# One of sixteen attention heads gets its transposes from VectorE in 32x32 blocks and its V product from 32-row matmuls

## The chip, the cores and the metric

The kernel runs on one core of a Trainium2 chip. The metric is device time in microseconds (us) of one execution, as the median of several runs. Engines: TensorE (PE for matmuls, PEld for weight loads), VectorE (DVE), ScalarE (ACT), GpSimd (POOL) and SyncE (SP), which issues most transfers.

## The reference, cut to what matters

Attention over 2 x 8 = 16 heads with 768 positions and 64 features each, masked by six-bit hash buckets, feeds two MLP stages. Only the attention is touched.

```python
mask = q_bucket[:, :, :, None] == k_bucket[:, :, None, :]
scores = np.where(mask, scale * np.matmul(q, k.transpose(0, 1, 3, 2)), -1000000000.0)
attn = np.exp(scores - np.max(scores, axis=-1, keepdims=True))
attn = attn / (np.sum(attn, axis=-1, keepdims=True) + 1e-09)
return np.matmul(attn, v).astype(np.float32)
```

## The kernel before, in words

The attention runs over 96 tiles, n = 0 to 95: six tiles of 128 queries for each head h = n // 6. For a tile, `t_qk` (lines 378 and 381) makes 128 x 768 scores with four matmuls into one of two PSUM tiles `s_ps`; the hash buckets enter through twelve extra rows of the operands `qb` and `hi`, so that unequal buckets become a large number. `t_max` (line 388, VectorE) clips the scores, takes the row extreme and writes the tile `p`; there are three of those. `t_exp` (line 400, ScalarE) takes exponentials in place and their row sum. `t_tr` (line 408, TensorE) transposes `p` in six blocks of 128 x 128 into two of the three PSUM banks `t` (`t_ps` twice and `pj_ps`), and `t_out` (line 417, ScalarE or VectorE) copies each bank into `pt`, keys on the partitions.

Three tiles make a group g of 384 queries, two groups a head. `block` runs once a group: `g_pv` (line 426) multiplies `pt` by V with six matmuls of 64 output rows, three into the upper half of the bank `u_ps` and three into the lower half, which `g_copy` (lines 448 and 451) takes out and `g_fold` adds up with transfers. Each 32-bit matmul shows in the profile as two instructions. In every second group `block` first makes the hash bits of the head two further on: two matmuls (line 352), two VectorE instructions `bits_rows` (line 359) right behind, and then a transfer `kb` (line 341, `hi<-q`), without which the scores of that head can't start.

TensorE's order in the attention is written out by hand in `names`: for each tile n the transposes of n, then the scores of n+3; behind the first tile of a group the V product of the group before. So `pv11` (with the bits of head 7) follows the scores of tile 39, and `pv13` (with the bits of head 8) the scores of tile 45; the scores of tile 48 are the first of head 8. The order on the other engines comes from a planner, `Work.run`, which simulates all engines at build time: it takes the task that could start first, and among those ready within 0.1 us (0.5 us on SP) the one with the earliest due time. Its prices and due times are the numbers in the `task` calls. Slots (`raw_s`) stand for buffers. Weight slices for the MLP are prepared by VectorE and ScalarE (`w_tick`, lines 201 to 224) wherever the planner finds room late in the attention.

Numbered by their order on the engines, tile 36 is the first of head 6: the scores of tile 39 start at 94.78 us in the profiled execution, those of tile 45 at 108.11 us and those of tile 48 at 115.16 us.

Of the kernel before, what the change touches and what calls it, by code (L numbers as in the profile page):

```python
# [18 lines left out]
DM, DF1, DF2 = 512, 768, 2048  # L19
NK = S // 128  # L20
CH = 256
HALF = S // 2
# [90 lines left out]
def lsh_attention_moe_kernel(  # L113
    ctx: ExitStack,
    tc: tile.TileContext,
    kq: bass.AP,
    v: bass.AP,
    pj: bass.AP,
    pc: bass.AP,
# [140 lines left out]
    def attention(mlp_steps):  # L260
        with ExitStack() as ax, ExitStack() as sx:
# [3 lines left out]
            p_p = ax.enter_context(tc.tile_pool(name="p", bufs=3))  # L265
            pt_p = ax.enter_context(tc.tile_pool(name="pt", bufs=3))
            sm_p = ax.enter_context(tc.tile_pool(name="sm", bufs=2))
# [11 lines left out]
            def load_head(h, parts=1):  # L279
                r = raw_p.tile([128, S], F32, tag="r", name="r")  # L280
                for i in range(parts):
                    cs = slice(i * S // parts, (i + 1) * S // parts)
                    nc.sync.dma_start(out=r[:, cs], in_=kq[h, :, cs])
                    if parts > 1 and i == 0:
                        nc.sync.dma_start(out=pj_raw, in_=pj)
                head[h] = dict(r=r)

            def load_v(h):
                vr = v_p.tile([128, NK, D], F32, tag="vr", name="vr", bufs=3)
                nc.sync.dma_start(out=vr, in_=v[h])  # L290
                head[h]["vr"] = vr

# [120 lines left out]
            def t_out(n, half, bank, copy):  # L413
                g, r = divmod(n, 3)
                if g not in grp:
                    grp[g] = pt_p.tile([128, NK, HALF], F32, tag="pt", name="pt")
                copy(  # L417
                    out=grp[g][:, 3 * half:3 * half + 3, r * 128:(r + 1) * 128],
                    in_=t_ps[bank.at][:, 0:HALF].rearrange("p (j q) -> p j q", j=3),
                )  # L420

# [133 lines left out]
            raw_s["vr"] = Slots(3)  # L555
# [41 lines left out]
            def bits_task(h, rows, due):  # L597
                q, ql, kh = moves[h]
                ready[h] = [task("SP", 0.8, due, prep_move, h, "kb", after=rows + [q], lag=2.5), q, ql, kh]

            def v_tasks(h):
                due = NK * h - 2
                vr = place("vr", 2)
                v_place[h] = vr
                if h > 0:
# [7 lines left out]
            def tile_tasks(n):  # L613
                h, t = divmod(n, NK)
                g, r = divmod(n, 3)
                sp, pp = place("s", 1), place("p", 2)
# [3 lines left out]
                if r == 0:  # L620
                    pt_p_[g] = place("pt", 1)
# [17 lines left out]
            def group_tasks(g, outs):  # L639
# [20 lines left out]
                )  # L660

            def pair_tasks(p_):
                due = 12 * p_ + 14
# [15 lines left out]
            for n in range(NT_):  # L679
                h, t = divmod(n, NK)  # L680
                if t == 0:
                    if h == 0:
                        v_tasks(0)
                        head_tasks(1)
                    if h + 2 < NH:
                        head_tasks(h + 2)
                    if h + 1 < NH:
                        v_tasks(h + 1)
                outs += tile_tasks(n)
                if n % 3 == 2:  # L690
# [6 lines left out]
            for g in range(NT_ // 3):  # L697
                for n in range(3 * g, 3 * g + 3):
                    names += [f"tr{n}", f"qk{n + 3}"]
                    if n == 3 * g and g:  # L700
                        names += [f"pv{g - 1}"] + ([f"rows{g // 4 - 1}"] if g % 4 == 2 else [])
            line = [t for x in names for t in order.get(x, ())]
# [249 lines left out]
```

## Time and profile before

| | us |
|---|---|
| median of 3 runs | 693.76 |
| lowest and highest | 693.68, 693.9 |
| the profiled execution | 694.73 |
| its span, first to last instruction | 693.0 |

The span is what the trace shows; the time of the same execution is 1.73 us longer and holds what lies around it. The runs without a profile lie about 1 us below the profiled one. The attention fills the span from about 9 to 232 us, the MLP the rest.

### The profile page before, as it was taken

Reading aid. Unit: us, or ns where it says so; the run is one execution under the profiler, and the core shown is the slowest. Engines: PE = TensorE matmul, PEld = TensorE weight load, DVE = VectorE, ACT = ScalarE, POOL = GpSimd, SP = SyncE. Lnnn points to the kernel's source line nnn. Section 1 sums busy time; section 2 is a strip of 40 time slices with the busy share of each in tenths; the row PEclk is TensorE's granted clock in tenths of the full one; section 3 lists DMA queues with packets and bytes.
Section 4 is the critical chain, followed back from the end, with each engine's and each line's share of the span. In section 5 each row is a group of like instructions: output and inputs, shape, how many; then the busy total and the mean of one; then the engine's idle time right before and its main releaser. Section 6 shows DMA issues by size and latency. Waiting matters only on the chain.

```text
span 693.0 us, 9878 instructions
## 1 busy us (share of the span) xinstructions
PE 683.4 (99%) x3516; PEld 541.3 (78%) x3516; DVE 491.3 (71%) x758; ACT 344.9 (50%) x669; POOL 273.0 (39%) x248
## 2 busy tenths in 40 slices
PE   7999999999999999999999999999999999999998
PEld 4777777677767688888888888888888888888886
DVE  6778787787776586775444356765888888888844
ACT  3777677777768333332322233665454444554430
POOL 4234564654730334443232112534434434434430
PEclk9999999999999999999999999999999999999999
DMA  5656576475541322221112022121111112211104
GB/s 157 131 135 142 138 195 159 115 177 140 141 101 39 107 92 91 92 92 53 47 45 69 31 70 88 56 78 45 61 61 62 61 61 66 85 62 61 31 0 183
DMA packets 26281, 62.76 MB, mean 91 GB/s; under 512 B 3940, under 2 KB 10692, under 8 KB 26232
## 3 DMA queue, kind: packets, MB, share of 16 engines
q1 hardware_dynamic: 26200, 62.12, 31.6%
q8 instruction: 28, 0.46, 0.3%
q14 instruction: 21, 0.17, 0.1%
q0 software_dynamic: 32, 0.00, 0.0%
HBM read 42.04 MB, written 3.19 MB: 65 GB/s over the span
## 4 chain that ended last, share of the span: by engine, by line
PE 94%; DVE 4%; ACT 1%; issue 1%; DMA 0%; DVEq 0%; ACTq 0%
PE b L746 47%; PE b L873 19%; PE u_ps L426 8%; PE t_ps L408 6%; PE s_ps L378 4%; PE s_ps L381 4%; PE pj_ps L408 3%; DVE p L388 1%; PE t_ps L352 1%; PE pj_ps L352 1%; DVE q L359 1%; DVE pt L417 1%; DVE lo L312 0%; ACT p L400 0%; DMA r<-in_kq 0%
## 5 line engine op out<-in xcount | busy, mean ns | idle before, releaser
L746 PE MATMUL b<-x_hl,w 128*128 128x512 f32 (+1 forms) x900 | 202.0, 381 | 0.0
L746 PEld LDWEIGHTS b<-x_hl,w 128*128 128x128 f32 x900 | 163.9, 188 | 33.1 <-issue 0.6
L773 POOL TENSOR_TENSOR g<-r,g 128x512 fp32r<-128x512 f32 x48 | 62.5, 1303 | 121.3 <-ACT g L772 121.3
L873 PE MATMUL b<-w,g 128*128 128x512 f32 (+1 forms) x438 | 105.9, 386 | 0.0
L388 DVE TENSOR_SCALAR_CACHE_REDUCE p<-s_ps 128x768 f32<-128x768 f32 x96 | 91.6, 956 | 15.8 <-PE s_ps L381 13.8
L400 ACT ACTIVATE p<-p,nm 128x768 f32<-128x768 f32 x96 | 90.1, 939 | 17.9 <-DVE p L388 16.9
L873 PEld LDWEIGHTS b<-w,g 128*128 128x128 f32 x438 | 81.5, 188 | 16.7
L230 POOL TENSOR_TENSOR w<-wg,w 128x512 fp32r<-128x512 f32 (+1 forms) x42 | 59.4, 1414 | 84.4 <-ACT w L224 68.6
L203 DVE SCALAR_TENSOR_TENSOR wg<-wg,wr 128x512 f32<-128x512 f32 (+1 forms) x58 | 66.1, 1140 | 35.6 <-ACT wg L201 34.8
L746 PE MATMUL b<-x_hl,wx 128*128 128x512 f32 x360 | 84.0, 389 | 0.0
L224 ACT CAST w<-wg 128x512 fp32r<-128x512 f32 (+1 forms) x42 | 25.5, 606 | 117.2 <-DVE wg L216 117.2
L746 PEld LDWEIGHTS b<-x_hl,wx 128*128 128x128 f32 x360 | 67.6, 188 | 14.0
L378 PE MATMUL s_ps<-lo,q 128*128 128x384 f32 x192 | 73.2, 381 | 3.5 <-DVE p L388 2.4
L426 PE MATMUL u_ps<-pt,vr 128*64 128x384 f32 x384 | 69.0, 491 | 0.2 <-DVE pt L417 0.2
L381 PE MATMUL s_ps<-hi,q 76*128 76x384 f32 x192 | 65.5, 341 | 0.7 <-DVE hi L343 0.7
L853 DVE SCALAR_TENSOR_TENSOR r<-r,b 128x512 f32<-128x512 f32 x48 | 33.0, 687 | 44.2 <-ACT r L852 44.2
L880 DVE TENSOR_TENSOR acc<-b,acc 128x512 f32<-128x512 f32 (+1 forms) x85 | 56.3, 675 | 7.7 <-PE b L873 7.6
L408 PE MATMUL t_ps<-ident,p 128*128 128x128 f32 x384 | 58.7, 275 | 0.3
L208 DVE TENSOR_SCALAR wg<-wg 128x512 int32<-128x512 int32 (+1 forms) x58 | 53.8, 927 | 2.8
L851 ACT ACTIVATE r<-b,half_sb 128x512 f32<-128x512 f32 x48 | 33.0, 687 | 41.3 <-PE b L746 41.3
L408 PEld LDWEIGHTS t_ps<-ident,p 128*128 128x128 f32 x384 | 45.8, 141 | 9.1 <-issue 4.8
L216 DVE SCALAR_TENSOR_TENSOR wg<-wr,wg 128x512 int32<-128x512 int32 (+1 forms) x58 | 51.7, 892 | 1.0
(87 smaller groups left out, 898.1 us busy)
## 6 DMA issues: line engine op xcount, KB each, us to landing
wr<-in_w SPq DMA_DIRECT2D x48, 512.0 KB
r<-in_kq SPq DMA_DIRECT2D x15, 384.0 KB
q<-hi SPq DMA_DIRECT2D x15, 384.0 KB
vr<-in_v SPq DMA_DIRECT2D x16, 192.0 KB
rb<-d SPq DMA_DIRECT2D x16, 192.0 KB
wr<-in_w SPq DMA_DIRECT2D x8, 384.0 KB
q<-lo SPq DMA_DIRECT2D x15, 192.0 KB
lo<-hi SPq DMA_DIRECT2D x15, 192.0 KB
```

What stands on the lines that cost most here:

```text
L203: nc.vector.scalar_tensor_tensor(out=f32(g), in0=f32(g), scalar=TINY_SQ, in1=f32(high), op0=ALU.is_ge, op1=ALU.mult)
L230: nc.gpsimd.tensor_tensor(out=w[:, 1, 0:cols], in0=f32(g2), in1=f32(w[:, 0, 0:cols]), op=ALU.subtract)
L378: nc.tensor.matmul(out=o, lhsT=hd["qa"][:, qs], rhs=hd["lo"][:, ks], start=True, stop=False)
L381: nc.tensor.matmul(out=o, lhsT=hd["qb"][0:76, qs], rhs=hd["hi"][0:76, ks], start=False, stop=True)
L388: nc.vector.tensor_scalar(out=p.rearrange("p (a k) -> p a k", a=2), in0=s_ps[n % 2][:, :, 0:HALF], scalar1=MASKED, scalar2=MASKED, op0=ALU ...
L400: nc.scalar.activation(out=p, in_=p, func=ACTF.Exp, scale=-1.0, bias=tl[n]["nm"], accum_out=pair[h // 2]["sums"][:, c:c + 1],)
L408: nc.tensor.transpose(out=t_ps[bank.at][:, j * 128:(j + 1) * 128], in_=tl[n]["p"][:, kt * 128:(kt + 1) * 128], identity=ident,)
L426: nc.tensor.matmul(out=u_ps[rows, 0:HALF], lhsT=vr[:, kt, :], rhs=grp[g][:, kt, :], start=(i == 0), stop=(i == 2),)
L746: nc.tensor.matmul(out=outp, lhsT=w_[a], rhs=x_[b_], start=(i == 0 and jj == 0), stop=(i == n - 1 and jj == 2),)
L773: nc.gpsimd.tensor_tensor(out=dst[:, 1, cs], in0=src, in1=f32(dst[:, 0, cs]), op=ALU.subtract)
L873: nc.tensor.matmul(out=pb[:, cs], lhsT=gs[f][:, a, tsl], rhs=wt[:, b_, cs], start=(n == 0), stop=(n == len(terms) - 1),)
L880: nc.vector.tensor_tensor(out=acc[:, t, cs], in0=pb[:, cs], in1=acc[:, t, cs], op=ALU.add)
```

## The change: what it does

For head 6 alone (`TURNED`), VectorE transposes each tile `p` of exponentials in 32x32 blocks into a new tile `dt` (`t_turn`): the blocks stay in their 32 partitions, so each quarter of the partitions holds the keys of its own 32 queries of every tile. The head's six tiles then have no `t_tr` and no `t_out`. V of that head is loaded once for each quarter (`v4`, 24 blocks of 32 keys, in all four quarters; 768 KB in place of 192 KB). `block4` makes the V product with 96 matmuls of 32 rows, 64 output columns and 192 moving columns: four quarters, each into a bank of its own (`u_ps` and the three `t` banks), even blocks into the upper and odd ones into the lower half. It comes in two parts, `b1` and `b2`; `b2` ends with the hash bits of head 8 as four matmuls of 192 columns into the free columns of two of the banks, and `rows4` takes those out in four instructions. `copy4` empties the four banks.

On TensorE `b1` stands behind the transposes of tile 42 and the scores of tile 45, `b2` behind the scores of tile 46 and ahead of the transposes of tile 43. The small transposes `rows` of each pair of heads move two tiles later. To make room, `pt` goes from three buffers to two, and V tiles of the other heads from three to two.

```diff
+            TURNED = (6,)
-                vr = v_p.tile([128, NK, D], F32, tag="vr", name="vr", bufs=3)
+                vr = v_p.tile([128, NK, D], F32, tag="vr", name="vr", bufs=2)
+            def load_v4(h):
+                vr = v_p.tile([128, NB, D], F32, tag="v4", name="v4", bufs=1)
+                nc.sync.dma_start(out=vr, in_=v4[h])
+            def t_turn(n):
+                nc.vector.transpose(out=head[h]["dt"][:, :, t * 32:(t + 1) * 32], in_=tl[n]["p"])
+            def block4(h, part, banks, bits):
+                for kb in range(part * NB // 2, (part + 1) * NB // 2):
+                    cols = UP if kb % 2 == 0 else DOWN
+                    for q in range(4):
+                        rows = slice(32 * q, 32 * q + 32)
+                        nc.tensor.matmul(
+                            out=b4_bank(banks[q])[cols, 0:NK * 32], lhsT=vr[rows, kb, :], rhs=dt[rows, kb, :],
+                            start=kb < 2, stop=kb >= NB - 2,
+                        )
+                if part and bits:
+                    for c in range(2):
+                        for half in range(2):
+                            nc.tensor.matmul(
+                                out=b4_bank(banks[c])[64 * half:64 * half + 64, 192:384], lhsT=pj_raw,
+                                rhs=head[bits]["r"][:, half * HALF + c * 192:half * HALF + c * 192 + 192], start=True, stop=True,
+                            )
+            def rows4(h, c, half, bank):
+                nc.vector.tensor_scalar(
+                    out=head[h]["qb"][64:108, at:at + 192], in0=b4_bank(bank)[rows, 192:384],
+                    scalar1=pc_sb[rows, 0:1], scalar2=pc_sb[rows, 1:2], op0=ALU.is_gt, op1=ALU.mult,
+                )
-            raw_s["pt"], raw_s["t"] = Slots(3), Slots(3)
+            raw_s["pt"], raw_s["t"] = Slots(2), Slots(3)
+                if turned:
+                    vready[h] = task("SP", 0.6, due - 2, load_v4, h, takes=[vr], lag=5.0)
+                if turned:
+                    return [task("DVE", 0.9, n - 4, t_turn, n, after=[ex], takes=[pt_p_[g]] if t == 0 else [], leaves=[pp])]
+                b1 = task("PE", 2.4, 6 * h + 8.4, block4, h, 0, banks, 0, after=outs + [vready[h]], takes=banks)
+                b2 = task(
+                    "PE", 3.4 if bits else 2.4, 6 * h + 8.4, block4, h, 1, banks, bits, after=[b1] + ([scaled[bits]] if bits else []),
+                names += [f"qk{n + 3}", f"pv{2 * h - 1}", f"tr{n}"] if after and t == 1 else [f"tr{n}", f"qk{n + 3}"]
+                if r == 0 and g and not (t and h in TURNED):
+                    names += [f"pv{2 * h - 2 if after and t == 0 else g - 1}"]
+                if g % 4 == 2 and t == 2:
+                    names += [f"rows{g // 4 - 1}"]
```

## Rows read from the trace of the kernel before

**Rows 1.** The page: busy us, share of the span and instructions by engine.
```profile
PE 683.4 (99%) x3516; PEld 541.3 (78%) x3516; DVE 491.3 (71%) x758; ACT 344.9 (50%) x669; POOL 273.0 (39%) x248
```

**Rows 2.** The page: the chain that ended last, shares of the span by engine.
```profile
PE 94%; DVE 4%; ACT 1%; issue 1%; DMA 0%; DVEq 0%; ACTq 0%
```

**Rows 3.** Timeline of PE about pv11: start, us, engine, line, instructions merged.
```profile
94.20 0.49 PE L408 MATMUL pj_ps<-ident,p 128*128 128x128 f32 x3
...
94.78 0.42 PE L378 MATMUL s_ps<-lo,q 128*128 128x384 f32 x1
...
95.66 0.87 PE L352 MATMUL t_ps<-r,pj_raw 128*64 128x384 f32 x4
96.35 2.10 PE L426 MATMUL u_ps<-pt,vr 128*64 128x384 f32 x12
98.39 0.55 PE L408 MATMUL pj_ps<-ident,p 128*128 128x128 f32 x3
```

**Rows 4.** Timeline of PE from the bits of head 8 to its first scores.
```profile
109.00 0.87 PE L352 MATMUL pj_ps<-r,pj_raw 128*64 128x384 f32 x4
...
112.42 0.42 PE L378 MATMUL s_ps<-lo,q 128*128 128x384 f32 x1
...
113.21 0.82 PE L408 MATMUL t_ps<-ident,p 128*128 128x128 f32 x6
...
115.16 0.42 PE L378 MATMUL s_ps<-lo,q 128*128 128x384 f32 x1
```

**Rows 5.** Timeline of DVE in head 6: start, us; in brackets idle time before.
```profile
88.15 0.96 DVE L388 TENSOR_SCALAR_CACHE_REDUCE p<-s_ps 128x768 f32<-128x768 f32 x1
...
89.03 0.56 DVE L417 COPY pt<-t_ps 128x384 f32<-128x384 f32 x1
89.50 0.95 DVE L388 TENSOR_SCALAR_CACHE_REDUCE p<-s_ps 128x768 f32<-128x768 f32 x1
...
94.41 0.96 DVE L388 TENSOR_SCALAR_CACHE_REDUCE p<-s_ps 128x768 f32<-128x768 f32 x1 [0.41 <-PE s_ps L381]
...
96.63 1.37 DVE L359 TENSOR_SCALAR q<-t_ps,pc_sb 44x384 fp32r<-44x384 f32 x2 [0.79 <-ACT p L400]
```

**Rows 6.** Windows: length, busy us (instructions) by engine, granted clock, DMA share, GB/s.
```profile
13.00:16.00 3.00, 1.54 (x9) 0.80 (x6) 2.92 (x5) 1.03 (x2) 1.60 (x2) 1.00 0.36 75
...
16.00:18.00 2.00, 1.54 (x10) 1.15 (x9) 1.97 (x5) 1.55 (x3) 0.00 (x0) 1.00 0.91 300
...
20.00:22.00 2.00, 2.00 (x17) 1.97 (x16) 1.70 (x4) 2.00 (x6) 0.62 (x1) 1.00 0.96 196
...
121.00:131.00 10.00, 8.54 (x55) 5.87 (x54) 9.36 (x17) 6.60 (x14) 7.70 (x10) 1.00 0.61 139
```

**Rows 7.** Groups by line and form: busy us, mean ns of one, idle before.
```profile
L388 DVE TENSOR_SCALAR_CACHE_REDUCE p<-s_ps 128x768 f32<-128x768 f32 x96 | 91.6, 956 | 15.8 <-PE s_ps L381 13.8 <-PE t_ps L408 0.6 <-ACT p L400 0.6
...
L426 PE MATMUL u_ps<-pt,vr 128*64 128x384 f32 x384 | 69.0, 491 | 0.2 <-DVE pt L417 0.2
...
L312 DVE SCALAR_TENSOR_TENSOR lo<-r,sc_sb,hi 128x384 fp32r<-128x384 f32 x4 | 3.7, 973 | 4.1 <-ACT hi L307 4.1
...
L343 DVE CAST q<-hi 64x384 fp32r<-64x384 f32 x2 | 0.7, 356 | 0.1
```

**Rows 8.** Timeline of SP's queue: issues of a V tile and of moves.
```profile
14.96 0.43 SPq L290 DMA_DIRECT2D vr<-in_v  x1
...
17.11 0.50 SPq L341 DMA_DIRECT2D lo<-hi  x1
...
99.57 0.59 SPq L462 DMA_DIRECT2D u<-uo  x1
...
111.37 0.80 SPq L341 DMA_DIRECT2D hi<-q  x1
```

**Rows 9.** Timeline of POOL: the sum that waits for that move.
```profile
101.89 1.01 POOL L471 TENSOR_TENSOR u<-u,uc 128x384 f32<-128x384 f32 x1 [1.76 <-DMA u<-uo]
```

**Rows 10.** Timeline of PE: the first scores of head 1.
```profile
21.66 0.42 PE L378 MATMUL s_ps<-lo,q 128*128 128x384 f32 x1
```

More of the change, by code (lines that the diff above doesn't have):

```diff
@@ L20 @@
 NK = S // 128
+NB = S // 32
 CH = 256
@@ L419, in t_out, with b4_bank, copy4 @@
                     in_=t_ps[bank.at][:, 0:HALF].rearrange("p (j q) -> p j q", j=3),
+                )
+            def t_turn(n):
+                h, t = divmod(n, NK)
+                if t == 0:
+                    head[h]["dt"] = pt_p.tile([128, NB, NK * 32], F32, tag="dt", name="dt", bufs=1)
+                nc.vector.transpose(out=head[h]["dt"][:, :, t * 32:(t + 1) * 32], in_=tl[n]["p"])
+            def b4_bank(b):
+                return u_ps if b.slots is raw_s["u_ps"] else t_ps[b.at]
+            def block4(h, part, banks, bits):
+                dt, vr = head[h]["dt"], head[h]["vr"]
+                for kb in range(part * NB // 2, (part + 1) * NB // 2):
[14 more added lines that the diff above has]
+            def rows4(h, c, half, bank):
+                rows = slice(64 * half, 64 * half + 44)
+                at = half * HALF + c * 192
+                nc.vector.tensor_scalar(
+                    out=head[h]["qb"][64:108, at:at + 192], in0=b4_bank(bank)[rows, 192:384],
+                    scalar1=pc_sb[rows, 0:1], scalar2=pc_sb[rows, 1:2], op0=ALU.is_gt, op1=ALU.mult,
+                )
+            def copy4(h, q, bank, copy):
+                pr = pair[h // 2]
+                if q == 0:
+                    pr["u"] = nm_p.tile([128, S], F32, tag="u", name="u")
+                copy(
+                    out=pr["u"].rearrange("p (t g k) -> p t g k", t=NK, g=4)[:, :, q, :],
+                    in_=b4_bank(bank)[:, 0:NK * 32].rearrange("p (t k) -> p t k", t=NK),
                 )
@@ L615, in tile_tasks @@
                 g, r = divmod(n, 3)
-                sp, pp = place("s", 1), place("p", 2)
+                turned = h in TURNED
+                sp, pp = place("s", 1), place("p", 1 if turned else 2)
                 tb = [place("t", 1) for i in range(2)]
@@ L619, in tile_tasks @@
                     sums_p[h // 2] = place("sums", 1)
-                if r == 0:
+                if turned and t == 0:
+                    pt_p_[g] = place("dt", 1)
+                elif r == 0:
                     pt_p_[g] = place("pt", 1)
@@ L660, in group_tasks, with turned_tasks @@
                 )
+            def turned_tasks(h, outs):
+                bits = h + 2 if h + 2 < NH else 0
+                banks = [place("u_ps", 3 if bits else 1)] + [place("t", 3 if bits and i == 0 else 1) for i in range(3)]
+                b1 = task("PE", 2.4, 6 * h + 8.4, block4, h, 0, banks, 0, after=outs + [vready[h]], takes=banks)
+                b2 = task(
+                    "PE", 3.4 if bits else 2.4, 6 * h + 8.4, block4, h, 1, banks, bits, after=[b1] + ([scaled[bits]] if bits else []),
+                    leaves=[pt_p_[2 * h], v_place[h]] + ([r_place[bits]] if bits else []),
+                )
+                order[f"pv{2 * h}"], order[f"pv{2 * h + 1}"] = [b1], [b2]
+                if bits:
+                    rows = [
+                        task("DVE", 0.45, 6 * h + 6, rows4, bits, c, half, banks[c], after=[b2], leaves=[banks[c]])
+                        for c in range(2) for half in range(2)
+                    ]
+                    bits_task(bits, rows, 6 * bits - 3)
+                u_p[h // 2], uc_p[h // 2] = place("u", 2), place("uc", 2)
+                cps = []
+                for q in range(4):
+                    ways = [("ACT", 0.43, nc.scalar.copy), ("DVE", 0.36, nc.vector.tensor_copy)]
+                    cps.append(task(*ways[0][:2], 6 * h + 5, copy4, h, q, banks[q], ways[0][2], after=[b2] + cps[:1], takes=[u_p[h // 2]] if q == 0 else [], leaves=[banks[q]]))
+                    work.also(*ways[1][:2], lambda a=(h, q, banks[q], ways[1][2]): copy4(*a), cps[-1])
+                for g in (2 * h, 2 * h + 1):
+                    adds[g] = task("SP", 0.5, 6 * h + 6, g_fold, g, after=cps, takes=[uc_p[h // 2]] if g % 2 == 0 else [], lag=3.5)
             def pair_tasks(p_):
@@ L696, in attention @@
             names = ["qk0", "qk1", "bits", "qk2"]
[L697 to L701, printed above, removed]
+            for n in range(NT_):
+                g, r = divmod(n, 3)
+                h, t = divmod(n, NK)
+                after = h - 1 in TURNED
+                names += [f"qk{n + 3}", f"pv{2 * h - 1}", f"tr{n}"] if after and t == 1 else [f"tr{n}", f"qk{n + 3}"]
[3 more added lines that the diff above has]
+                    names += [f"rows{g // 4 - 1}"]
             line = [t for x in names for t in order.get(x, ())]
```

24 lines of the change are left out of this document (16 added, 8 removed).

## The prediction, made before the changed kernel ran

> **What bounds the kernel now.** I read the page's busy times first: TensorE is busy 99% of the span, VectorE 71% [rows 1]. The chain that ended last is TensorE for 94% [rows 2]. So time saved on TensorE counts, if nothing else takes its place, and VectorE is the engine with the least room beside it. Then I read TensorE's and VectorE's timelines about head 6. TensorE goes from transposes to scores to V product without a gap: six transposes take 0.58 us (94.20 to 94.78), the bits of a head 0.69 us (95.66 to 96.35), a V product 2.04 us (96.35 to 98.39) [rows 3], the scores of a tile 0.79 us (112.42 to 113.21) [rows 4]. VectorE runs close on its heels: the check of tile 38 starts when its scores end, after 0.41 us of idling [rows 5]. Last I read the windows: from 121 to 131 us TensorE is busy 8.54 of 10 us while VectorE is busy 9.36 [rows 6]. Here, where VectorE also prepares weights, TensorE already waits for it, 1.46 us in all.
>
> **TensorE's account.** Removed are six tiles of transposes, 6 x 0.58 = 3.5 us, and two V products, 2 x 2.04 = 4.1 us: 7.6 us. The bits stay at the same number of columns, 0.7 us. Added are 96 matmuls of half the columns, 192 instructions. The trace shows no matmul of 32 rows, so I bound them. In the V product 12 instructions take 2.04 us though one lasts 491 ns [rows 3, 7]; the upper and the lower half run side by side, six pairs of 0.34 us. At half the columns a pair takes 0.17 us. If all eight parts of the array (four quarters, two halves) run side by side, each has 24 instructions one after the other: 24 x 0.17 = 4.1 us. If only the two halves do and the quarters queue, it is 96 x 0.17 = 16.3 us. I take 4.6 us, near the lower end, because the nearest row has its two parts fully side by side; 2.3 us for each part. TensorE's own account then gains 3.0 us, which would be 690.8.
>
> [...]
>
> **What TensorE waits for instead.** For head 6 TensorE has only scores to make, and scores wait for free `s_ps`, so for VectorE's checks. On VectorE a check holds the engine 0.88 us (88.15 to 89.03), a copy 0.47 us (89.03 to 89.50) [rows 5]. A turn is not in the trace. Bounds: twice the cheapest 384-column row from SBUF to SBUF, 2 x 0.356 = 0.71 us, and twice the dearest, 2 x 0.973 = 1.95 us [rows 7]. I take 0.88 us, that of the check, which has the same 128 x 768 elements. So VectorE gives up copies (at most two a tile, one on average since ScalarE shares them) and takes a turn.
>
> Count from 94.41 us, where the check of tile 38 starts [rows 5]. `b1` stands behind the scores of tile 45, which need the check of tile 43, and needs all six turns. VectorE owes six checks (5.3 us), five turns (4.4 us; I let the first one fall into idle time before), the bits of head 7 (1.37 us) and the wait ahead of them that is there now (0.79 us) [rows 5]: 11.9 us, up to 106.3. The scores of tile 45 take it to 107.1. TensorE alone would be there at 103.1: its V product would end 0.58 us earlier, at 97.8, then six scores, 4.7 us, and one tile's transposes, 0.58 us. So some 4 us of waiting appears where 7.6 us of work is taken out: the work on TensorE is moved behind VectorE instead of beside it.
>
> Behind it: `b1` to 109.4, scores of tile 46 to 110.2, `b2` to 112.5, bits of head 8 to 113.2.
>
> **The next wait is the key bits of head 8.** Now the bits start at 109.00 and the first scores of head 8 at 115.16 [rows 4]. Between them lie 6.2 us. In the changed order the bits are the last of `b2`, and only the transposes of tiles 43, 44 and 45 (1.7 us) and the scores of tile 47 (0.8 us) stand between. The chain beside it: the rows begin 0.97 us after the bits start (95.66 to 96.63) [rows 3, 5], so at 113.5. Four instructions of half the columns cost between 0.34 us (half of 0.68) and 0.68 us each; I take 0.45, nearer the half: 115.3. Then the move. Its issue follows the rows at once now (111.37) [rows 8], and a similar move took 2.3 us from issue to the first instruction that uses it (99.57 to 101.89) [rows 8, 9]. That is 117.6 for the scores of tile 48. TensorE alone, with 0.5 us for a bank to be emptied behind `b2`, would be there at 116.3. So TensorE waits 1.3 us more, and tile 48 stands at 117.6 where it stood at 115.16: 2.4 us late.
>
> **The start.** The planner has room for one more V tile ahead (14.96, V of head 2) [rows 8]. With two buffers that tile must wait, and the load of `v4` has no condition, so it takes that place: 768 KB for 192 KB, 590 thousand bytes more. At 196 to 300 GB/s [rows 6] that is 2.0 to 3.0 us more in a queue that is busy 0.91 to 0.96 of those windows. Behind it stands the last move for head 1, issued at 17.11 [rows 8], and head 1's first scores start at 21.66 [rows 10]. With 2.3 us for a move there are 2.2 us to spare, so the scores come between 0 and 0.8 us late; I take 0.3.
>
> **What is given back.** VectorE and ScalarE run up to two tiles ahead during `b1` and `b2`, and the weight steps that cost TensorE 1.46 us between 121 and 131 us [rows 6] may slip there. Between 0 and 1.46; I take half, 0.7.
>
> **Free edits.** `pt` with two buffers: the V product of the group before last is done two tiles before the buffer is written again. Two V tiles: by the order of the V products a slot comes free nine tiles ahead of its next use. The later `rows` and `copy4` (4 copies for 2) end nothing on the chain; without that cover a copy costs its 0.47 us, which the 0.5 us above holds. [...]
>
> **Sum.** 2.4 + 0.3 - 0.7 = +2.0 us. Against the profiled execution the span goes from 693.0 to 695.0 and its time from 694.73 to 696.7. The median of runs lies 1 us under the profiled time, so the forecast is 693.76 + 2.0 = 695.8.
>
> **Rivals.**
> - No measurable change. The small terms lie at their lower ends: block 4.1 us (-0.5), rows 0.34 us each (-0.4), no start cost (-0.3), all 1.46 us given back (-0.8). That is 2.0 us off: 693.8. For it speaks that the order was left room between `b1` and `b2`; against it that it needs most of them.
> - Faster: VectorE is not the bound. If a turn is short enough, TensorE waits for nothing and `b1` starts at 103.1, 4.0 us earlier: -2.0, 691.8. Each 0.1 us off a turn brings five turns 0.5 us forward, so the loss is gone at 0.48 us a turn, and 0.2% is gained at 0.20 us. The cheapest row gives 0.71 us [rows 7], which is against it. [...]
> - Far slower: the four quarters don't run side by side. At 16.3 us the block adds 11.7 us: 707; halfway 701. Or the turn is as dear as the dearest row, 1.95 us: 5 x 1.07 = 5.4 us more, 701. The clock falling in the stretch of waits would end there too.
>
> **How the numbers follow.** The forecast, a wait for VectorE's turns and then for the bits, has 0.48 (its own range 694.9 to 697.5); no measurable change 0.26; VectorE not the bound 0.13; quarters or turn far dearer 0.13. 0.2% is 1.4 us, about what a measurement of this kernel can tell from none. Slower takes the forecast and the last, but 0.01 of it: 0.60; same 0.27; faster 0.13. The range leaves out most of the fast case below 692.4 and most of the dear case above 699.0.
>
> **What would show it.** Right: idle TensorE between the scores of tiles 40 to 45, released by the check; `b1` near 107 us; the 192 instructions in about 4.6 us; a wait for the move `hi<-q` ahead of tile 48. Wrong: turns under 0.5 us, TensorE without gaps there, or blocks of more than 4 us each.

## The result, and the profile after

The changed kernel takes 699.07 us (median of 3 runs, 697.85 to 699.22) where the kernel before takes 693.76: a ratio of 1.0071, with a 95% interval of 1.0048 to 1.0094, so 3.3 to 6.5 us slower. The forecast was slower, 695.8 us; the median lies 0.07 us above the upper end of the range. The profiled execution took 697.85 us with a span of 696.1; before it was 694.73 and 693.0. Of the changed kernel's three runs it is the one with the highest mean granted clock, 0.993; the two others show 0.990: more of their time lies at a lowered clock.

The page of the changed kernel, busy us by engine and the chain that ended last:

```profile
PE 683.8 (98%) x3652; PEld 542.9 (78%) x3652; DVE 493.5 (71%) x761; ACT 343.6 (49%) x664; POOL 273.5 (39%) x248
...
PE 95%; DVE 3%; issue 1%; ACT 1%; DMA 1%; DVEq 0%; ACTq 0%
```

Against [rows 1] TensorE was to lose 3 us of work. Its busy time is the same, 683.8 for 683.4. Busy is not work: part of it ran at half the clock, which the windows show (length, busy us of PE, PEld, DVE, ACT and POOL, granted clock, DMA share, GB/s):

```profile
14.50:17.90 3.40, 3.35 (x12) 3.26 (x13) 3.20 (x6) 1.89 (x5) 0.23 (x1) 0.50 0.96 311
97.00:103.30 6.30, 4.61 (x24) 2.53 (x20) 6.01 (x11) 2.74 (x7) 5.62 (x7) 1.00 0.74 149
103.30:110.10 6.80, 4.93 (x16) 4.33 (x17) 5.94 (x11) 3.52 (x7) 4.92 (x6) 0.50 0.60 176
110.10:115.80 5.70, 5.70 (x201) 4.64 (x200) 3.08 (x6) 2.07 (x5) 0.00 (x0) 1.00 0.41 104
121.00:131.00 10.00, 9.77 (x61) 6.25 (x61) 7.70 (x17) 7.19 (x15) 6.95 (x8) 1.00 0.73 184
```

Read the second and the third row together. From 97.0 to 103.3 us TensorE had work for 4.61 of 6.30 us; then the granted clock is 0.50 for 6.8 us. The timeline of PE in the same stretch (start, us, in brackets idle time ahead and what ended it) shows what this does:

```profile
98.79 0.44 PE L386 MATMUL s_ps<-lo,q 128*128 128x384 f32 x1
...
101.32 0.44 PE L386 MATMUL s_ps<-lo,q 128*128 128x384 f32 x1 [1.57 <-DVE p L396]
...
103.35 0.69 PE L386 MATMUL s_ps<-lo,q 128*128 128x384 f32 x1 [0.16 <-DVE p L396]
...
106.81 0.69 PE L386 MATMUL s_ps<-lo,q 128*128 128x384 f32 x1 [1.82 <-DVE p L396]
...
108.26 1.48 PE L416 MATMUL t_ps<-ident,p 128*128 128x128 f32 x6
109.39 0.67 PE L386 MATMUL s_ps<-lo,q 128*128 128x384 f32 x1
...
110.59 0.37 PE L445 MATMUL u_ps<-dt,v 32*64 32x192 f32 x1
...
110.63 0.38 PE L445 MATMUL t_ps<-dt,v 32*64 32x192 f32 x2
110.80 0.32 PE L445 MATMUL u_ps<-dt,v 32*64 32x192 f32 x1
...
115.77 0.55 PE L452 MATMUL u_ps<-r,pj_raw 128*64 128x192 f32 x4
...
121.23 0.44 PE L389 MATMUL s_ps<-hi,q 76*128 76x384 f32 x1 [0.63 <-DMA hi<-q]
```

Two waits for VectorE's checks (1.57 and 1.82 us) stand ahead of the scores of tiles 41 and 44. The six transposes of tile 42 take 1.13 us (108.26 to 109.39) where six took 0.58 [rows 3]. The block, the 192 short matmul instructions of `b1` and `b2`, starts at 110.59. Eight of them start from 110.59 to 110.63, the next eight from 110.80 on: all eight parts run side by side. Each half of the block is twelve such rounds and takes 2.13 us up to the instruction behind it (110.59 to 112.72 and 113.64 to 115.77). At the end stands the wait for the move `hi<-q`.

The timeline of DVE (VectorE) shows who is late; L396 is the check, L434 the turn, L367 and L460 take out the hash bits:

```profile
97.03 1.37 DVE L367 TENSOR_SCALAR q<-pj_ps,pc_sb 44x384 fp32r<-44x384 f32 x2 [0.86 <-ACT p L408]
98.43 1.84 DVE L434 STREAM_TRANSPOSE dt<-p 128x768 f32<-128x768 f32 x2
100.30 0.96 DVE L396 TENSOR_SCALAR_CACHE_REDUCE p<-s_ps 128x768 f32<-128x768 f32 x1
...
103.21 2.69 DVE L434 STREAM_TRANSPOSE dt<-p 128x768 f32<-128x768 f32 x3
105.83 0.92 DVE L396 TENSOR_SCALAR_CACHE_REDUCE p<-s_ps 128x768 f32<-128x768 f32 x1
...
106.68 0.95 DVE L396 TENSOR_SCALAR_CACHE_REDUCE p<-s_ps 128x768 f32<-128x768 f32 x1
...
116.77 0.97 DVE L460 TENSOR_SCALAR q<-u_ps,pc_sb 44x192 fp32r<-44x192 f32 x2 [0.43 <-ACT u L469]
117.76 0.97 DVE L460 TENSOR_SCALAR q<-pj_ps,pc_sb 44x192 fp32r<-44x192 f32 x2
```

VectorE makes the bits, then two turns, then the check of tile 39; later it makes three turns in a row ahead of the check of tile 42 at 105.83. A turn takes VectorE 0.9 us. The check of tile 43, the one at 106.68, ends at 107.55.

Along the kernel, all from the same timeline: the first scores of head 1 start at 22.35 us (21.66 before [rows 10]); those of tile 36, the first of head 6, 0.80 us late; those of tile 48 at 120.17, 5.0 us late [rows 4]; the MLP 3.1 us late. The rest of the kernel lasts the same.

### The profile page after: what moved, and what is told of

Same layout as the page of the kernel before. It is cut to its first block, busy times and chain, and to the rows that moved or that the text cites. A ratio compares the mean times of both kernels' runs of the same rounds, so it can differ in the third digit from the quotient of the medians.

```text
span 696.1 us, 10143 instructions
## 1 busy us (share of the span) xinstructions
PE 683.8 (98%) x3652; PEld 542.9 (78%) x3652; DVE 493.5 (71%) x761; ACT 343.6 (49%) x664; POOL 273.5 (39%) x248
## 4 chain that ended last, share of the span: by engine, by line
PE 95%; DVE 3%; issue 1%; ACT 1%; DMA 1%; DVEq 0%; ACTq 0%
PE b L838 47%; PE b L965 19%; PE u_ps L478 9%; PE t_ps L416 6%; PE s_ps L386 5%; PE s_ps L389 5%; PE pj_ps L416 3%; PE pj_ps L360 1%; PE t_ps L360 1%; DVE dt L434 1%; PE u_ps L445 0%; DVE lo L320 0%; DVE q L367 0%; DVE p L396 0%; DMA hi<-q 0%
## 5 line engine op out<-in xcount | busy, mean ns | idle before, releaser
L396 DVE TENSOR_SCALAR_CACHE_REDUCE p<-s_ps 128x768 f32<-128x768 f32 x96 | 91.6, 956 | 17.6 <-PE s_ps L389 13.8
L226 ACT CAST w<-wg 128x512 fp32r<-128x512 f32 (+1 forms) x42 | 25.5, 606 | 117.1 <-DVE wg L218 117.1
L386 PE MATMUL s_ps<-lo,q 128*128 128x384 f32 x192 | 75.1, 391 | 5.7 <-DVE p L396 4.9
L389 PE MATMUL s_ps<-hi,q 76*128 76x384 f32 x192 | 66.9, 348 | 1.1 <-DMA hi<-q 0.6
L478 PE MATMUL u_ps<-pt,vr 128*64 128x384 f32 x360 | 64.8, 491 | 0.2 <-DVE pt L425 0.2
```

Source lines behind the costliest of these rows:

```text
L386: nc.tensor.matmul(out=o, lhsT=hd["qa"][:, qs], rhs=hd["lo"][:, ks], start=True, stop=False)
L389: nc.tensor.matmul(out=o, lhsT=hd["qb"][0:76, qs], rhs=hd["hi"][0:76, ks], start=False, stop=True)
L396: nc.vector.tensor_scalar(out=p.rearrange("p (a k) -> p a k", a=2), in0=s_ps[n % 2][:, :, 0:HALF], scalar1=MASKED, scalar2=MASKED, op0=ALU ...
L478: nc.tensor.matmul(out=u_ps[rows, 0:HALF], lhsT=vr[:, kt, :], rhs=grp[g][:, kt, :], start=(i == 0), stop=(i == 2),)
```

## The experiments

Each ratio is to runs of the kernel before in the same series, whose medians lie from 693.66 to 694.01 us. The columns in the middle are starts on TensorE in the profiled execution, counted from the scores of tile 33, so that what the start of the kernel adds drops out. They come from one execution each: before and e1_none, which turn no head, differ by 1.1 us at tile 72. The block counts from its first short matmul; in e2_early_bits and e2_all the bits stand ahead of it.

| kernel | median us | ratio to before (95%) | block | tile 48 | tile 72 | clock at half level, 60 to 130 us |
|---|---|---|---|---|---|---|
| before | 693.76 | 1 | - | 33.8 | 89.8 | none |
| changed | 699.07 | 1.0071 (1.0048 to 1.0094) | 28.4 | 38.0 | 92.5 | 6.8 us |
| e1_none | 693.49 | 0.9994 (0.9984 to 1.0004) | - | 33.9 | 88.7 | none |
| e1_checks_first | 698.81 | 1.0063 (1.0050 to 1.0076) | 27.7 | 39.4 | 94.5 | 6.8 us |
| e1_fill | 698.17 | 1.0058 (1.0043 to 1.0074) | 26.5 | 38.6 | 92.8 | none |
| e1_twice | 705.87 | 1.0167 (1.0152 to 1.0182) | 34.9 | 46.6 | 101.3 | 13.7 us |
| e2_short_turn | 696.40 | 1.0040 (1.0026 to 1.0053) | 25.6 | 36.0 | 92.2 | 3.4 us |
| e2_early_bits | 699.29 | 1.0075 (1.0058 to 1.0093) | 30.2 | 42.6 | 96.5 | 13.7 us |
| e2_order_fill | 696.76 | 1.0041 (1.0026 to 1.0055) | 26.5 | 37.1 | 92.4 | none |
| e2_all | 697.84 | 1.0056 (1.0039 to 1.0074) | 27.3 | 40.1 | 93.8 | 3.4 us |
| e3_spread_a | 693.69 | 0.9991 (0.9979 to 1.0003) | 32.7 | 31.1 | 87.9 | none |
| e3_spread_b | 695.29 | 1.0015 (1.0002 to 1.0028) | 33.2 | 31.6 | 89.5 | none |
| e4_apart | 691.12 | 0.9951 (0.9936 to 0.9967) | 32.7 | 31.1 | 87.6 | none |
| e4_apart_late | 693.10 | 0.9981 (0.9968 to 0.9995) | 32.7 | 31.1 | 87.4 | none |

**The edits around the turned head alone.** No head is turned; the buffers, the later `rows` and the order stay as changed.

```diff
-            TURNED = (6,)
+            TURNED = ()
```

> No head is turned; the two buffers fewer, the later small transposes and the unused v4 input stay. If the loss comes from head 6 (VectorE's turns, the clock, the bits), this is the kernel before again: 693.8 us within 0.7. If the edits to buffers and order cost something by themselves, it lies 1 us or more above 693.8.

No difference from before. The two `pt` buffers, the two V tiles and the moved `rows` cost nothing. Its profiled execution has 88.7 us from tile 33 to tile 72, where that of before has 89.8.

**Checks ahead of turns.** The planner puts a turn behind the checks that wait.

```diff
-                    return [task("DVE", 0.9, n - 4, t_turn, n, ...
+                    return [task("DVE", 0.9, n + 6, t_turn, n, ...
```

> The turns get a later due time (n + 6 for n - 4), so the planner puts VectorE's checks ahead of them; the work is the same. If the order on VectorE costs (three turns in a row hold up the check of tile 42), the first part of the block starts 2 to 3 us earlier than 110.6 us and the time falls by 1.5 to 3 us against the changed kernel. If VectorE's total alone or the clock alone sets it, the block starts within 0.7 us of 110.6 and the time stays within 0.7.

The check of tile 42 comes earlier, but the block starts only 0.8 us earlier after tile 33, not 2 to 3. The clock still falls for 6.8 us, and the time is the same as with the change. The order of VectorE alone is not it.

**Idle matmuls for the clock.** 33 matmuls of bf16 zeros between the scores of tiles 40 to 44, and the planner counts every bank that a task takes, so that they get one; the rest of the work is as in the change, but the planner's order on VectorE comes out differently.

```diff
+            need = sum(x.slots is p.slots for x in task["takes"])
-            if not p.slots.free:
+            if len(p.slots.free) < need:
...
+            FILL = {37: 12, 38: 3, 39: 3, 40: 12, 41: 3}
+                order[f"fill{n}"] = [task("PE", 0.11 * count, n, lambda: warm_up(count, bp.at), takes=[bp], leaves=[bp])]
-                names += [..., f"tr{n}", f"qk{n + 3}"]
+                names += [..., f"tr{n}", f"fill{n}", f"qk{n + 3}"]
```

> TensorE gets 33 small matmuls without use (0.11 us each at full clock) between the scores of tiles 40 to 44, where it waits. [...] If VectorE alone sets the start of the block, the clock may stay up but the time falls by less than 0.5 us.

The windows of this kernel for the two stretches read above:

```profile
97.00:103.30 6.30, 6.30 (x49) 4.69 (x45) 6.04 (x11) 2.62 (x6) 5.43 (x7) 1.00 0.65 167
103.30:110.10 6.80, 6.37 (x119) 4.89 (x117) 5.45 (x11) 5.36 (x12) 3.63 (x4) 1.00 0.59 156
```

its timeline of DVE, where turns (L436) and the checks (L398) of tiles 41, 42 and 43 now alternate:

```profile
101.19 0.98 DVE L436 STREAM_TRANSPOSE dt<-p 128x768 f32<-128x768 f32 x1 [0.22 <-ACT p L410]
102.09 0.92 DVE L398 TENSOR_SCALAR_CACHE_REDUCE p<-s_ps 128x768 f32<-128x768 f32 x1
...
103.84 0.92 DVE L398 TENSOR_SCALAR_CACHE_REDUCE p<-s_ps 128x768 f32<-128x768 f32 x1
...
105.59 0.92 DVE L398 TENSOR_SCALAR_CACHE_REDUCE p<-s_ps 128x768 f32<-128x768 f32 x1
```

and its timeline of PE behind the check of tile 43 and behind the block:

```profile
106.59 0.43 PE L388 MATMUL s_ps<-lo,q 128*128 128x384 f32 x1
...
107.47 0.37 PE L447 MATMUL u_ps<-dt,v 32*64 32x192 f32 x1
...
115.89 0.55 PE L418 MATMUL t_ps<-ident,p 128*128 128x128 f32 x3 [1.57 <-DVE u L471]
```

The clock stays at 1.00, and the block starts at 107.47. The check of tile 43 ends 18.4 us after the scores of tile 36, as with the change (18.3): VectorE is no faster. What has gone is the time from that check to the block, 1.0 us (106.44 to 107.47) instead of 3.0 (107.55 to 110.59). Not all of these 2.0 us are the clock. With checks and turns alternating, the scores of tile 44 and the transposes of tile 42 are out of the way when the scores of tile 45 may start (106.59); in the change they last until 109.39. The clock's part can be read in the change itself: the scores of tile 44, six transposes and the scores of tile 45 take 3.78 us there (106.81 to 110.59), and at full clock 0.79 + 0.58 + 0.79 = 2.16 us [rows 3, 4]. So the clock costs some 1.6 us ahead of the block, the order the rest. But the 2.0 us do not reach the end: tile 48 comes 38.6 us after tile 33, no better than 38.0. The two halves of the block take 2.72 and 2.36 us here, and a wait of 1.57 us for a bank stands behind it, where the change had 0.16. The time lies 0.9 us under the change by the ratios, with intervals that overlap: between the author's estimate for the clock as a cause, 1 to 1.6 us, and the less than 0.5 for VectorE alone.

**Every turn made twice.** The second one writes the same data again, and the planner's price doubles to 1.8.

```diff
-                nc.vector.transpose(out=head[h]["dt"][:, :, t * 32:(t + 1) * 32], in_=tl[n]["p"])
+                for _ in range(2):
+                    nc.vector.transpose(out=head[h]["dt"][:, :, t * 32:(t + 1) * 32], in_=tl[n]["p"])
```

> Each turn is made twice, so VectorE has six more of 0.89 us; the result is the same. If VectorE's turns are on the path to the block, the time rises by 4 to 6 us against the changed kernel. If they are hidden, by less than 1 us.

6.8 us more than the change, above the 4 to 6 expected, for some 5.3 us more on VectorE (6 x 0.89). Its timeline of DVE shows six turns in a row ahead of one check, and that of PE the 4.83 us that TensorE waits for this check:

```profile
106.06 5.73 DVE L435 STREAM_TRANSPOSE dt<-p 128x768 f32<-128x768 f32 x6
111.71 0.92 DVE L396 TENSOR_SCALAR_CACHE_REDUCE p<-s_ps 128x768 f32<-128x768 f32 x1
...
112.70 0.69 PE L386 MATMUL s_ps<-lo,q 128*128 128x384 f32 x1 [4.83 <-DVE p L396]
```

The turns are on the path, and with the longer waits the stretch at half level is twice as long (13.7 us for 6.8).

**Short turns.** The turn is cut to two of 24 blocks. The kernel leaves out the rest: those parts of `dt` are zeros that GpSimd writes early. The planner's price for a turn falls to 0.2, so its order on VectorE changes too.

```diff
-                nc.vector.transpose(out=head[h]["dt"][:, :, t * 32:(t + 1) * 32], in_=tl[n]["p"])
+                nc.vector.transpose(out=head[h]["dt"][:, 0:2, t * 32:(t + 1) * 32], in_=tl[n]["p"][:, 0:64])
```

> Leaves work out: only the first 64 of the 768 columns of each tile of head 6 are turned, the rest of dt is zeros written early by GpSimd; everything else (block, rows, moves, order) is as in the change. If VectorE's turning time is what costs (my theory): a turn of 0.15 us or less, no clock fall near 103 us, block4 starts 14 to 15.5 us after the scores of tile 36 (21.4 with full turns), tile 48 26 to 28 us after them (30.9 with full turns, 26.7 before), 692.5 to 694.5 us in all. Rival, the block and what follows it cost as much by themselves (emptying of the banks, bits, move): block4 earlier too, but tile 48 still 29.5 us or more after tile 36 and 696.5 us or more.

My theory fell here, though the rival's figures are not quite reached either (tile 48 28.9 us after tile 36, where it said 29.5). With turns of 0.24 us the kernel is still 2.7 us slower than before (interval 1.8 to 3.7). Its runs with a granted clock of 1.000 take 694.91 to 695.95 us, the others, at 0.992 to 0.998, up to 698.47. The timeline of DVE:

```profile
101.57 0.24 DVE L432 STREAM_TRANSPOSE dt<-p 128x64 f32<-128x64 f32 x1 [0.81 <-ACT p L408]
101.74 0.92 DVE L396 TENSOR_SCALAR_CACHE_REDUCE p<-s_ps 128x768 f32<-128x768 f32 x1
```

and of PE:

```profile
102.73 0.57 PE L386 MATMUL s_ps<-lo,q 128*128 128x384 f32 x1 [1.29 <-DVE p L396]
...
113.76 0.85 PE L416 MATMUL t_ps<-ident,p 128*128 128x128 f32 x6 [1.14 <-DVE u L472]
```

The turn of tile 41 stands ahead of the check of tile 42 and waits 0.81 us for ScalarE's exponentials; the check waits behind it, TensorE waits 1.29 us for the check, and the clock is at half level from 102.9 for 3.4 us. What stops TensorE here is not how much VectorE has to do. The scores of tile 42 end at 100.73 and VectorE idles from 100.76 on, but their check starts at 101.74, behind the turn that waits for ScalarE, and TensorE has nothing but scores to do. Tile 48 comes 2.1 us earlier than with the change, tile 72 only 0.3 us: three waits of 0.79, 0.41 and 0.35 us follow behind tile 48.

**Bits of head 8 at the start of the block.** They move from the end of the second half to the start of the first, the rows beside the block.

```diff
+                if bits:
+                    for c in range(2):
...
                 for kb in range(part * NB // 2, (part + 1) * NB // 2):
...
-                if part and bits:
-                    for c in range(2):
...
-                        task("DVE", 0.45, 6 * h + 6, rows4, bits, c, half, banks[c], after=[b2], leaves=[banks[c]])
+                        task("DVE", 0.45, 6 * h + 6, rows4, bits, c, half, banks[c], after=[b1], leaves=[banks[c]])
```

> The bits of head 8 come first in the first half of the block, so the rows and the move run beside the second half. If the wait for the move hi<-q (0.6 us ahead of tile 48) and the rows on VectorE behind the block count: tile 48 0.6 to 1.5 us nearer to tile 36 than 30.9, 698 us. Rival, the emptying of the three t banks behind the second half paces the transposes of tiles 43 and 44 whatever the bits do: 30.5 to 31 us, 698.8 to 699.2, the wait for hi<-q gone from TensorE's timeline and longer waits for banks in its place. The clock falls near 103 us as in the change by both.

The rival was right, and more: the wait for `hi<-q` is gone, and two waits for banks stand in its place in the timeline of PE.

```profile
118.35 0.55 PE L416 MATMUL pj_ps<-ident,p 128*128 128x128 f32 x3 [1.53 <-ACT u L469]
...
120.25 0.55 PE L416 MATMUL t_ps<-ident,p 128*128 128x128 f32 x3 [1.02 <-DVE u L469]
```

The second one is long because VectorE makes weight steps from 117.92 to 119.8 before it empties the last bank. The clock is at half level longer than with the change (13.7 us in two stretches), so the start of the block can't be compared.

**Order and idle matmuls together,** and **both with the early bits.**

```diff
+            FILL = {37: 8, 38: 6, 39: 6, 40: 6, 41: 6}
-                    return [task("DVE", 0.9, n - 4, t_turn, n, ...
+                    return [task("DVE", 0.9, n + 6, t_turn, n, ...
```

> Checks of the scores are put ahead of turns, and 32 idle matmuls between the scores of tiles 40 to 44 keep TensorE busy. If the clock alone spoilt the run with checks ahead (698.81, block4 early but at half clock): clock 1.00 there, block4 18.5 to 19.5 us after tile 36, tile 48 29.5 to 30.5, 696.8 to 697.8 us. Rival, the banks and the bits behind the block bind: tile 48 at 31 or more whatever the clock, 698 or more.

> Checks ahead of turns, idle matmuls for the clock and the bits of head 8 at the start of the block, together. If each takes away a wait of its own: tile 48 at 28.5 to 29.5 us after tile 36 and 695.5 to 696.8 us, still not faster than the kernel before since VectorE's turning time is left. Rival, they take away the same wait or only move it to the banks: no better than the best of the three alone, 697.5 or more.

The first behaves as expected up to tile 48 (37.1, and 696.76 us), but at tile 72 it is where the change is (92.4). The 1.3 us by which its profiled execution is the shorter one (696.53 for 697.85) are nearly all there at tile 33 (80.95 for 82.15), ahead of the turned head. With the early bits it is worse: the rival was right there. Six kernels took away waits of different kinds, and none gets below 92.2 us from tile 33 to tile 72, where kernels with no turned head need 88.7 and 89.8.

**The turns put where TensorE has other work.** Not a wait is removed now, but the load is moved. Head 6's exponentials are kept: `dt` itself holds four raw tiles, two more stand in weight buffers that are not in use yet. The turns run beside the transposes of head 7, the V products of groups 10 and 11 are cut in three and put between the scores of head 6, the bits of heads 7 and 8 come by themselves, and the block waits until the scores of tile 49. The planner counts banks as in e1_fill and gets other prices for tiles 33 to 59. All this changes together, so no part of it has a price of its own. The order on TensorE is written out (e3_spread_b has another one):

```diff
+            SPLIT, TURNAT, TDUE = ((10, 11), [39, 43, 44, 45, 46, 47], 4)
+            EXTRA = {33: 'tr33 bits7 qk36 qk37 tr34 pv10.0 qk38 pv10.1 pv10.2 qk39 qk40 tr35 qk41 pv11.0 qk42 qk43 pv11.1 pv11.2 qk44 tr42 qk45 tr43 qk46 bits8 tr44 qk47 tr45 tr46 rows2 pv14 tr47 qk48 qk49 pv12 pv13 qk50 qk51 tr48 pv15 ...
-                nc.vector.transpose(out=head[h]["dt"][:, :, t * 32:(t + 1) * 32], in_=tl[n]["p"])
+                nc.vector.transpose(out=head[h]["dt"][:, TO[t], :], in_=tl[n]["p"])
-                            out=b4_bank(banks[q])[cols, 0:NK * 32], lhsT=vr[rows, kb, :], rhs=dt[rows, kb, :],
+                            out=b4_bank(banks[q])[cols, 0:NK * 32].rearrange("p (t k) -> p t k", t=NK), lhsT=vr[rows, kb, :],
+                            rhs=dt[rows, :, 32 * kb:32 * kb + 32],
```

> The same block and the same six turns, but put elsewhere: exponentials of head 6 are kept (dt holds six tiles, two more stand in weight buffers not yet used), turns come one by one after the checks of tiles 39 and 43 to 47, beside the transposes of head 7, the V products of groups 10 and 11 are cut in three between the scores of head 6, the bits of heads 7 and 8 come by themselves, and both halves of the block follow the scores of tile 49. If the loss is VectorE's load all at one place, where TensorE has little else to do: clock 1.00 throughout, from the scores of tile 33 to those of tile 72 87 to 88.3 us (89.8 before, 88.7 in the kernel with no head turned, 92.5 with the change), time 691 to 693 us, faster than before. Rival, TensorE's saving of 3.5 us can't be had because VectorE and ScalarE are full over the whole of heads 6 to 8 and the emptying of the banks costs 1 to 2 us in any place: 89 us or more and 693.5 to 696 us.

> As e3_spread_a with another order: the turns after the checks of tiles 37, 43 and 45 to 47 (two there), V products of groups 10 and 11 spread more evenly, bits of head 8 behind the scores of tile 46. By the first theory 87 to 88.5 us from tile 33 to tile 72 and 691 to 693 us, by the rival 89 or more and 693.5 to 696 us; the difference between the two orders is under 1 us by either.

The same six turns and the same block: tile 72 comes 4.6 us earlier than with the change in the first, 3.0 in the second. By its interval the first is not to be told from before. But its five runs with a granted clock of 1.000 take 691.38 to 692.94 us, and those of before in the same series with 0.999 or 1.000 693.25 to 694.41; its other seven runs show 0.994 to 0.998, and the profiled one of them has its half-level stretch at the start, from 16.3 us on. The second meets the rival's figures and lies 1.5 us behind the first at tile 72, where under 1 was expected. One gap stays in its timeline of PE, in the middle of the second half of the block, which follows the first half at once (in the second kernel the gap is 2.20 us):

```profile
119.14 0.32 PE L460 MATMUL pj_ps<-dt,v 32*64 32x192 f32 x1 [1.17 <-issue]
```

**Scores between the halves,** and **the load of `v4` held back.**

```diff
-  ... qk49 pv12 pv13 qk50 qk51 ...
+  ... qk49 pv12 qk50 pv13 qk51 ...
```

```diff
-                    vready[h] = task("SP", 0.6, due - 2, load_v4, h, takes=[vr], lag=5.0)
+                    vready[h] = task("SP", 0.6, due - 2, load_v4, h, takes=[vr], lag=5.0, after=[exps[20]])
```

> As e3_spread_a, with the scores of tile 50 between the two halves of the block. There the halves stood together, and TensorE stood still for 1.17 us in the middle of the second one with nothing that the trace shows to wait for; with scores between them (the change) no such gap was seen. If the row of some 400 short instructions without a pause is what runs dry: no gap, 86.3 to 87 us from the scores of tile 33 to those of tile 72 (87.9 in e3_spread_a), 692 to 693 us, faster than before. Rival, the gap comes from what the DMA queues carry just then (weights) and stays wherever the block's second half falls at that time: 87.5 us or more, 693.4 to 694.2 us.

> As e4_apart, with the load of v4 held back until the exponentials of tile 20 instead of falling among the first loads. If those 768 KB at the start cost what the prediction's start term says (0.3 us, at most 0.8): 0.2 to 0.8 us less than e4_apart. Rival, the start varies by itself (scores of tile 6 between 20.4 and 22.4 us in kernels with and without v4) and the load costs nothing: the same as e4_apart within 0.3 us.

e4_apart is faster than both kernels: 691.12 us in five runs, 2.3 to 4.4 us under before by its interval. All five show a granted clock of 1.000; runs of before in this series with 0.999 or 1.000 take 692.49 us or more, the longest of the five 691.79. Its windows about head 6 and the block:

```profile
95.00:105.00 10.00, 10.00 (x60) 6.84 (x58) 9.23 (x19) 8.83 (x21) 7.82 (x10) 1.00 0.80 186
105.00:115.00 10.00, 9.82 (x147) 7.29 (x145) 9.52 (x18) 6.56 (x17) 5.52 (x6) 1.00 0.65 175
115.00:125.00 10.00, 8.88 (x142) 6.06 (x135) 7.66 (x12) 5.12 (x13) 7.43 (x7) 1.00 0.35 76
```

TensorE is busy 10.00 and 9.82 of 10 us at clock 1.00 while VectorE is busy 9.23 and 9.52: both engines are full at once. But its own reason was wrong: the gap is still there, 1.12 us, so keeping the halves apart did not close it. Most of its lead over e3_spread_a is the start (scores of tile 6 at 20.36 and 22.01 us in the profiled executions); from tile 33 to tile 72 it is 0.3 us ahead. Holding `v4` back saves nothing, and neither expectation met the 2.0 us that the kernel loses by it. In the profiled execution the start is slow there too (22.03 us, with a stretch at half level from 16.6 us on), though `v4` is no longer in it, and the load now stands in the queue ahead of the move of the key bits of head 5, which TensorE waits 0.98 us for, at 76.87.

## Why the prediction was right in sign and short in size

The forecast was 3.3 us short (699.07 for 695.8). Against the profiled execution it was 1.1 us short (697.85 for 696.73). The other 2.2 us come from carrying the sum over to the median: the profiled execution of before lies 1.0 us above its median, that of after 1.2 us under its own, where the two longer runs show the lower granted clock (0.990 for 0.993). The 1.1 us are 1.8 us more at tile 48, 0.4 more at the start, 0.1 between the start and tile 36, and 1.2 more given back.

- **Tile 48: +2.4 forecast, +4.2 measured** (5.0 less the 0.8 that stand at tile 36 already). VectorE's count held: 11.9 us from the check of tile 38 to the end of that of tile 43, 12.4 measured (95.20 to 107.55). So did the turn: 0.88 forecast, 0.86 to 0.90 apart measured in a row. By itself a turn of 768 columns lasts 0.97 us, and one of 64 columns in e2_short_turn 0.24: some 1.04 ns for each further column. The block took 2.13 us a half, 4.3 us in all, near the lower bound of 2.05 a half, for the 2.3 taken. From the start of the block to the instruction that uses the move it was 10.6 us for 10.5, so that instruction came 2.8 us later than forecast: 0.5 from VectorE's count, 2.2 from the check of tile 43 to the block, 0.1 behind it. The first matmul of tile 48 does not need the move and stands 1.06 us ahead of it. (By its own terms the prediction has TensorE alone at tile 48 at 116.2, not 116.3; the time of 117.6 does not hang on it.)
- **The step that failed is TensorE's clock, for which the sum has no term.** From the check of tile 43 to the block the prediction had 0.8 us, the scores of tile 45. It was 3.0, with the granted clock at 0.50. Some 1.6 us of the difference are the clock. The other 0.6 are order: three turns in a row push the check of tile 42 right ahead of that of tile 43, so the scores of tile 44 and the transposes of tile 42 are not done when it ends. In e1_fill, with the clock kept and turns and checks alternating, it is 1.0. In the kernel before, the clock was at 1.00 in a stretch with TensorE busy 1.54 of 3.00 us [rows 6]; one such row does not show that the next stretch stays, and in the changed kernel 4.61 of 6.30 us busy were followed by 0.50 for 6.8 us.
- **The start: +0.3 forecast, +0.7 measured, and not by the mechanism named.** The window from 14.5 to 17.9 us is at half level. That comes and goes: it is in e3_spread_a, not in e1_fill or e4_apart with the same early load of `v4`, and it is in e4_apart_late without it. What brings it is not shown.
- **Given back: 0.7 forecast, 1.9 measured** between tile 48 and the MLP. From 121 to 131 us TensorE is busy 9.77 of 10, 8.54 before [rows 6]. The reason I gave, that weight steps slip into the time of the block, is not shown: e1_none, without a block, has no such waits either. Of the 1.46 us, 0.83 are a gap in the timeline of PE of before that the trace puts down to "issue", not to VectorE:

```profile
130.67 0.42 PE L378 MATMUL s_ps<-lo,q 128*128 128x384 f32 x1 [0.83 <-issue]
```

Whether these waits belong to the kernel before or to that one execution, no run tells.

The rivals. That the quarters queue is out: eight parts start within 0.04 us. That a turn under 0.48 us would bring the loss to nothing is out as well: at 0.24 us it is still 2.7 us. There the prediction let TensorE reach the block at 103.1 once VectorE is no longer the bound; but scores, check, exponentials and turn make a chain across three engines, in which the check of tile 42 stood 1.0 us behind a waiting turn in e2_short_turn (100.73 to 101.74), and in head 6 nothing else is left on TensorE to fill it. "The clock falling", named as a way to some 701 us, was a part of it, at a price of some 1.6 us ahead of the block. It is not the whole loss: the runs of e1_fill and e2_order_fill with a granted clock of 0.999 or 1.000 take 696.45 to 698.01 us, such runs of before in the same two series 692.11 to 694.24.

So where did the 3.3 us of TensorE's work go (7.6 us removed, 4.3 added)? From tile 33 to tile 72 the change needs 92.5 us, 2.7 more than before and 3.8 more than e1_none. The windows of this stretch, in the changed kernel, in e1_none and in e4_apart:

```profile
82.15:174.62 92.47, 87.96 (x718) 63.73 (x716) 74.77 (x143) 63.37 (x140) 48.29 (x53) 0.96 0.60 149
...
80.18:168.87 88.69, 88.10 (x582) 63.38 (x580) 70.73 (x140) 64.50 (x145) 48.75 (x53) 1.00 0.63 157
...
80.16:167.80 87.64, 86.34 (x713) 61.70 (x712) 72.72 (x139) 63.21 (x142) 49.52 (x53) 1.00 0.63 158
```

With the change TensorE is busy 87.96 us, part of it at half the clock, and idle for 4.5. In e1_none it is busy 88.10 and idle for 0.6, in e4_apart busy 86.34 and idle for 1.3. The work that was taken out is just what TensorE had to do between the scores of head 6, and the block takes all four banks, so that no transposes run beside it or before the banks are empty. What one wait gives up the next one takes: the check, the clock, the banks, the move. Spreading the same work got 4.8 of the us back (87.6). That can't be the planner's new prices alone: a perfect order of the work of e1_none, whose TensorE is idle for 0.6 us only, would still need 88.1. The saving that shows there is 1.8 us of TensorE's busy time, not 3.3; where the rest is, no run tells.

## What to carry to other kernels

Work taken from the bounding engine paid here only where that engine had something else to do at that very place; where it had only work that waits for the other engine, its busy time turned into waits and into a lower clock (with the change 4.5 us idle from tile 33 to tile 72, and 6.8 us at 0.50). Before removing one wait after the other, move the load: here the same turns beside the next head's transposes, with V products cut up to fill the gaps, made a loss of 5.3 us into a gain of 0.8 to 2.8 (e4_apart_late and e4_apart). And give the clock a term of its own in the sum: 3.4 us (e2_short_turn) to 13.7 us (e1_twice) at half level stood behind such waits here.

## What the runs showed of the hardware

**The clock fell behind waits inside a busy kernel.** In the changed kernel, after 97 to 103.3 us with 4.61 of 6.30 us busy and a wait of 1.57 us in it, it was at half level for 6.8 us; in e1_twice for 13.7 us, with a wait of 3.60 us ahead of that and one of 4.83 us in it. In e1_fill, with TensorE kept busy 6.30 of 6.30 us by idle matmuls, it stayed at 1.00.

**Eight parts of the array at once.** Four quarters of 32 rows by two halves of 64 columns: in the changed kernel eight matmuls of 192 columns start within 0.04 us, the later rounds 0.16 to 0.17 us apart. Where nothing stands between the halves (e3_spread_a) the first half takes 2.00 us.

**A gap inside a row of short instructions.** In the second half of the block TensorE stood still for 1.17, 2.20, 1.12 and 0.95 us in e3_spread_a, e3_spread_b, e4_apart and e4_apart_late, with nothing that the trace shows to wait for, and for 0.57 us in e2_all; in the changed kernel there is none. The gap keeps to a place in TensorE's row of instructions and not to a time: it stands behind the 840th of all matmul instructions in the four e3 and e4 kernels and behind the 843rd in e2_all. That is behind the 151st of the block's 192 in e3_spread_a and e3_spread_b, and behind the 147th in e4_apart and e4_apart_late, where the scores of tile 50, four instructions, stand between the halves. In the changed kernel the 840th lies behind the block, among the transposes. The window from the start of e4_apart up to the gap counts the 840. The view of the DMA queues, from 115.7 to 117.1 us, has one packet of instructions just ahead of the gap, and the timeline of PE the gap itself:

```profile
0.00:118.00 118.00, 114.53 (x840) 81.76 (x841) 90.80 (x183) 81.09 (x174) 55.65 (x69) 1.00 0.63 160
...
q8 instruction: 1, 0.02, 5.8%
...
118.55 0.38 PE L460 MATMUL t_ps<-dt,v 32*64 32x192 f32 x2 [1.12 <-issue]
```

The last matmul ahead of the gap starts at 117.10 and lasts 0.32 us, the next one starts at 118.55. The packet holds 0.02 MB; those of the same queue in the traces of before and of the changed kernel hold 16,384 bytes each. A half of the block is 96 matmuls and 96 weight loads in some 2 us. That the instructions behind the gap came too late is the author's guess from the packet, the fixed place and the order of the times, and it was not shown: e1_fill and e2_order_fill have their 840th matmul instruction in the second half of the block too, and no such gap.
